# mLSTM into two MoE layers on one core: output gates by tanh, 1 + tanh in VectorE's product, and a new early order

## The chip, the cores and the metric

The kernel runs on one core of a Trainium2 chip. The metric is the device time in microseconds (us) of one execution. Engines are named as in the profile: PE is TensorE (matmuls), DVE is VectorE, ACT is ScalarE, POOL is GpSimd, SP is SyncE, which here issues most of the DMA transfers.

## The reference

The input is q, k, v (2 batches, 8 heads, 768 steps, 40 wide) and three gates. The first part is an mLSTM, the second a layer without a nonlinearity between its matrices but with a product, the third a layer with Mish. Everything is float32.

```python
for t in range(S):
    m_new = np.maximum(f_gate[:, :, t] + m, i_gate[:, :, t])
    f_stab = np.exp(f_gate[:, :, t] + m - m_new)
    i_stab = np.exp(i_gate[:, :, t] - m_new)
    m = m_new
    C = f_stab * C + i_stab * einsum('bhd,bhe->bhde', vt, kt)
    n = f_stab * n + i_stab * kt
    h_tilde = einsum('bhde,bhe->bhd', C, qt)
    denom = maximum(abs(n . qt), 1.0)
    o = 1.0 / (1.0 + exp(-o_gate[:, :, t]))
    y[:, :, t] = o * h_tilde / denom
x = y as 1536 tokens x 320
h = ((x @ w1) * (x @ w2)) @ w3 @ w_out     # 320 -> 1024 -> 1024 -> 320
h2 = h @ w_in                              # 320 -> 2048
out = (h2 * tanh(softplus(h2))) @ w_out2   # 2048 -> 320
```

## The kernel before

**Precision.** PE multiplies at full speed only in a rounded kind of float32 (`fp32r` in the rows). Where both factors are long, each is split into a high part that is exact in that kind and a low part, and a product is made of two or three matmuls. Splitting a weight tile (`add_piece`) takes a load (line 481), the magnitude (487 on ACT or 489 on DVE), a clamp (493), three bit operations (497, 502, 507) on DVE, the high part by ACT (512) and the low part by a subtraction (the helper `tt`, line 410) on DVE or POOL. All two-operand instructions that go through `tt` carry line 410; they are told apart by their tiles.

**Attention.** The 768 steps of a batch are cut into 6 chunks of 128; with 2 batches this gives 12 units u, chunk u // 2, batch u % 2. A unit goes through these steps, each a node of `add_unit`:

- `E` (623, 624, PE): exponents of the 128 x 128 decays into PSUM, two banks. For the first `mu` units a product with `causal` adds the mask (623); for the others POOL masks the result by an affine select (634). `dw` (629, ACT) takes the exponential and gives `w`.
- `S` (650, PE): the scores; `wg` (410, DVE, two halves): `w<-psS,w`, scores times decays.
- `vw` (410, POOL): values times the last decays; `U` (675, PE) and `st` (410, 692, DVE): the state that goes on to the next chunk of the batch; `I`, `dx`, `Ie` (661, 664, 639, 410): what comes from the state.
- `Y` (699, PE): 16 small matmuls in full fp32, `cb` (410 or 711, DVE): `y`, the numerator and the denominator. `r1` (716, ACT) its magnitude, `r2` (719, DVE) the maximum with 1, `r3` (722, DVE) the reciprocal.
- `xs` (410, POOL): `x<-y,sg`, the numerator times the output gate; `xo` (410, POOL): times `r`; `dup` (736, ACT); `X` (743, PE): transposition into `psX`; `Xe`, `Xl` (748 and 410): high part `hs`, low part `ls`.

The gates `sg` are loaded as six tiles of 2 chunks of a batch (`add_sigmoids`, 814: a sigmoid on ACT, two tiles and then four in a row). There are fewer places than tiles, so a later load waits until a tile has been read by `xs` of both its units. Sigmoid and exponential lie in different tables of ACT; whenever ACT goes from one to the other, a table is loaded.

**Start.** `start` computes the exponents' rows from the two gates on DVE by scans, for three pieces of the sequence (first, second and the other four chunks): `pa` (879), `pt` (410), `pb` (895), `pc` (900), `less` (927, DVE, what has to be subtracted), `lr` (905, ACT, a rounding), `ll` (410, DVE, its remainder), `rb` (919 or 410, `ex_r`) and `lb` (935, `ex_l`), the two factors of E.

**Layers.** Tokens go in 3 blocks of 512 (2 chunks of both batches). For each block the products A and B (1057, `psa`, `psb`, 8 slices of 128 of w1 and w2), `Ae` (1072, ACT) and `Be` (410, DVE, `a<-psb,a`), `Ph`, `Pl`. Once, the weights w3 and w_out are multiplied (W, 1028) from the parts `th` of w3 and `wol` of w_out; then X1 (1097 to 1102), and for groups of eight slices H (1186), Mish on ACT (1191, 1195), and O (1210), which is copied and stored.

**What sets the order.** The whole order is planned when the kernel is built: the class `Work` holds nodes with an engine, a length, what they need and what they free, and picks for each engine the ready node with the lowest due time. The due times of attention, of the first weights and of A and B come from a table of numbers (`DUE`), the choice of engines from `ENG`, other constants from `TUNE`. Where the plan expects PE to idle for long, it puts in fillers (`keep_warm`, 594: products of `causal` and `identr` into `psz` that nobody reads). Every engine then runs its instructions in the planned order, and so does SP its transfers.

Of the kernel before, what the change touches and what calls it, by code (L numbers as in the profile page):

```python
# [19 lines left out]
NQK = 2  # L20
# [6 lines left out]
    sgg=(2, 4), mu=8, s_pe=0.268, s_act=0.543, s_dve=0.435, s_pool=0.206, ahead=1, w0n=5, ff=0.972, gd=0.0,  # L27
    ph=0.071, a0=-12.81, ap=-93.853, a_ld=-1652.39, e_e=8363.2, e_s=3345.95, e_r=2252.59, g_ld=6316.58,
# [3 lines left out]
    c_o2=88.35, cp_o2=12.531, c_wi=-5894.32, c_o3=-2264.6, m0=232.0, grp=8, mp0=-162.897, mp=204.465, m_o=1263.83,  # L32
# [3 lines left out]
    mag_w12='ACT', mag_wo='ACT', mag_w3='ACT', mag_wi='DVE', mag_o2='DVE', mag_o3='DVE', lo_w12='DVE', lo_wo='DVE',  # L36
    lo_w3='POOL', lo_wi='POOL', lo_o2='DVE', lo_o3='DVE', xo='POOL', vw='POOL', dup='ACT', rb0='DVE', rc0='DVE',
    rb1='DVE', rc1='DVE', rb='ACT', rc='ACT', st0='DVE', cb0='DVE', prep='ACT', g_tt='DVE', g_ll='DVE',
    lo_w120='DVE', lo_w121='DVE', lo_w122='DVE', lo_w123='DVE', lo_w124='DVE', lo_w125='POOL', lo_w126='DVE',
# [25 lines left out]
    bits2_1=61.7, mag_3=32.5, X_3=47.0, X_2=46.7, r2_4=44.8, dw_7=46.5, vw_5=43.9, r3_4=46.6, U_4=46.2,
    clamp_3=34.4, Xe_3=46.9, U_5=41.3, wg_5=50.4, Xe_2=46.5, sgm_2=47.7, ld_qk_7=31.4, st_5=50.7, Y_5=50.2,
    vw_6=49.9, ld_kv_7=41.9, st_4=32.2, Xl_3=43.0, S_6=52.6, cb_5=61.2, Xl_2=50.6, E_8=20.7, r1_5=45.6, xs_4=51.3,
    sgm_3=51.8, sgm_4=51.8, sgm_5=51.8, wg_6=52.0, A_0=53.4, dw_8=53.9, xs_5=49.6, ld_kv_8=25.3, r2_5=31.3,
    bits1_3=47.6, r3_5=49.7, vw_7=60.1, B_0=55.3, bits2_3=65.5, Ae_0=45.8, bits_1=62.5, I_7=66.9, ld_kv_9=56.1,
# [284 lines left out]
def dve(n):  # L354
    return 0.07 + n / 960
# [991 lines left out]
```

## Time and profile before

| | before |
|---|---|
| median of 3 runs | 418.12 us (418.02 to 418.21) |
| the profiled execution | 418.2 us |
| its span, first to last instruction | 416.5 us |
| mean granted clock of PE | 0.998 |
| busy: PE, DVE, ACT, POOL | 409.5, 291.1, 197.7, 80.4 us |
| share of the span | 98%, 70%, 47%, 19% |

The rows further down give times in us from the first instruction. A row of a timeline or of the chain can hold several instructions in a row of the same kind (`x2`); its second number is then the time from the first's start to the last's end. PE takes up a matmul before the one ahead has ended, so the distance between two starts, not the length, is what one costs. What stands in brackets at a row's end is the time the engine stood idle before, and what ended it.

### The profile page before, as it was taken

Reading aid. Unit: us, or ns where it says so; the run is one execution under the profiler, and the core shown is the slowest. Engines: PE = TensorE matmul, PEld = TensorE weight load, DVE = VectorE, ACT = ScalarE, POOL = GpSimd, SP = SyncE. Lnnn points to the kernel's source line nnn. Section 1 sums busy time; section 2 is a strip of 40 time slices with the busy share of each in tenths; the row PEclk is TensorE's granted clock in tenths of the full one; section 3 lists DMA queues with packets and bytes.
Section 4 is the critical chain, followed back from the end, with each engine's and each line's share of the span. In section 5 each row is a group of like instructions: output and inputs, shape, how many; then the busy total and the mean of one; then the engine's idle time right before and its main releaser. Section 6 shows DMA issues by size and latency. Waiting matters only on the chain.

```text
span 416.5 us, 7129 instructions
## 1 busy us (share of the span) xinstructions
PE 409.5 (98%) x2815; PEld 359.8 (86%) x2815; DVE 291.1 (70%) x527; ACT 197.7 (47%) x381; POOL 80.4 (19%) x78
## 2 busy tenths in 40 slices
PE   8999999999999999999999999999999999999996
PEld 5689988798888899988888888989989999889995
DVE  7999999999899969779999987789231041330221
ACT  8787967444544444542644376157051161340430
POOL 3234264345102242431001132300000000000000
PEclk9999999999999999999999999999999999999999
DMA  7957744433313543445243253420100000100002
GB/s 238 324 178 220 239 119 153 139 97 127 114 50 102 168 136 101 150 139 166 65 104 87 64 127 90 164 63 2 65 0 2 0 2 2 63 2 0 2 2 64
DMA packets 30497, 40.88 MB, mean 98 GB/s; under 512 B 1856, under 2 KB 24640, under 8 KB 30464
## 3 DMA queue, kind: packets, MB, share of 16 engines
q1 hardware_dynamic: 29952, 39.95, 31.4%
q8 instruction: 22, 0.36, 0.4%
q10 hardware_dynamic: 512, 0.48, 0.4%
q14 instruction: 11, 0.09, 0.1%
HBM read 38.45 MB, written 1.97 MB: 97 GB/s over the span
## 4 chain that ended last, share of the span: by engine, by line
PE 93%; DVE 5%; DMA 1%; ACT 0%; issue 0%; DVEq 0%
PE pso L1210 21%; PE psh L1186 20%; PE psb L1057 11%; PE psa L1057 10%; PE psw L1028 7%; PE psY L699 5%; PE psS L650 3%; PE psx L1097 3%; PE psx L1099 3%; PE psx L1098 3%; PE psI L661 2%; PE psx L1102 1%; PE psx L1101 1%; PE psE L624 1%; DVE gates L410 1%; PE psX L743 1%
## 5 line engine op out<-in xcount | busy, mean ns | idle before, releaser
L410 DVE TENSOR_TENSOR gl<-u,gh 128x512 fp32r<-128x512 f32 x48 | 32.9, 691 | 68.7 <-ACT u L1195 68.7
L1191 ACT ACTIVATE gh<-psh 128x512 fp32r<-128x512 f32 x48 | 28.8, 601 | 79.5 <-PE psh L1186 79.4
L1186 PE MATMUL psh<-xd,wih 64*128 64x512 f32 x240 | 59.4, 395 | 0.0
L1186 PEld LDWEIGHTS psh<-xd,wih 64*128 64x128 f32 x240 | 43.1, 184 | 3.6 <-ACT u L1195 0.2
L1210 PE MATMUL pso<-wo,gh 128*128 128x320 f32 x192 | 42.6, 310 | 0.0
L1186 PE MATMUL psh<-hs,wih 64*128 64x512 f32 x144 | 41.6, 395 | 0.0
L502 DVE SCALAR_TENSOR_TENSOR f<-raw,f 128x640 int32<-128x640 int32 (+2 forms) x44 | 40.0, 908 | 0.9
L507 DVE SCALAR_TENSOR_TENSOR f<-raw,f 128x640 int32<-128x640 int32 (+2 forms) x44 | 37.7, 858 | 0.9
L410 POOL TENSOR_TENSOR th<-f,th 128x512 fp32r<-128x512 f32 x16 | 22.1, 1381 | 62.1 <-ACT th L512 59.1
L1210 PEld LDWEIGHTS pso<-wo,gh 128*128 128x128 f32 x192 | 32.0, 188 | 1.1 <-issue 1.1
L1186 PE MATMUL psh<-xd,wil 64*128 64x512 f32 x120 | 31.6, 391 | 0.0
L1186 PE MATMUL psh<-hs,wil 64*128 64x512 f32 x120 | 31.4, 391 | 0.0
L1210 PE MATMUL pso<-wo2h,gh 128*128 128x320 f32 x96 | 30.0, 312 | 0.0
L1210 PE MATMUL pso<-wo2h,gl 128*128 128x320 f32 x96 | 29.6, 309 | 0.0
L1210 PE MATMUL pso<-wo2l,gh 128*128 128x320 f32 x96 | 29.6, 309 | 0.0
L1210 PE MATMUL pso<-wo,gl 128*128 128x320 f32 x96 | 29.6, 309 | 0.0
L1057 PE MATMUL psa<-hs,w12h 128*128 128x512 f32 x72 | 28.9, 401 | 0.1
L1195 ACT ACTIVATE u<-psh 128x512 f32<-128x512 f32 x48 | 28.9, 603 | 0.0
L1057 PE MATMUL psb<-hs,w12h 128*128 128x512 f32 x72 | 28.3, 394 | 0.2 <-DVE y L410 0.2
L1186 PEld LDWEIGHTS psh<-hs,wih 64*128 64x128 f32 x144 | 25.7, 184 | 3.2 <-issue 1.3
L1028 PE MATMUL psw<-woh,th 128*128 128x320 f32 x128 | 28.5, 310 | 0.0
L493 DVE TENSOR_SCALAR f<-f 128x640 f32<-128x640 f32 (+2 forms) x44 | 23.6, 536 | 7.0 <-ACT f L487 6.3
(146 smaller groups left out, 1031.8 us busy)
## 6 DMA issues: line engine op xcount, KB each, us to landing
raw<-in_w_dram SPq DMA_DIRECT2D x16, 512.0 KB
raw<-in_w_out_dram SPq DMA_DIRECT2D x12, 640.0 KB
raw<-in_w_dram SPq DMA_DIRECT2D x16, 384.0 KB
raw<-in_w_in_dram SPq DMA_DIRECT2D x16, 320.0 KB
kv<-in_kv_dram SPq DMA_DIRECT2D x12, 324.0 KB
qk<-in_qk_dram SPq DMA_DIRECT2D x24, 160.0 KB
sg<-in_o_gate_dram SPq DMA_DIRECT2D x12, 160.0 KB
out_dram<-yo SPq DMA_DIRECT2D x9, 160.0 KB
```

Of the source, the lines that this page charges most:

```text
L410: return eng.tensor_tensor(out=o, in0=a, in1=b, op=op)
L493: nc.vector.tensor_scalar(out=ff, in0=ff, scalar1=HI_MIN, scalar2=HI_MAX, op0=ALU.max, op1=ALU.min)
L502: nc.vector.scalar_tensor_tensor(out=f, in0=t["raw"][:, :, 1], scalar=-0x40000000, in1=f, op0=ALU.bitwise_and, op1=ALU.bitwise_or)
L507: nc.vector.scalar_tensor_tensor(out=f, in0=t["raw"][:, :, 0], scalar=29, in1=f, op0=ALU.logical_shift_right, op1=ALU.bitwise_or)
L650: nc.tensor.matmul(t["S"][g][:, p * T:(p + 1) * T], lhsT=t["qk"][rows, 1, p, :], rhs=t["qk"][rows, 0, p, :], start=True, stop=True)
L699: nc.tensor.matmul(ps[:, h * VW:(h + 1) * VW], lhsT=t["w"][:, h, :], rhs=t["v"][:, h, :], start=True, stop=True)
L1028: nc.tensor.matmul(ps, lhsT=t[a][:, 0, c * 128:(c + 1) * 128], rhs=wo[b], start=(c0 + c + s == 0), stop=(c0 + c == KC - 1 and s == 2))
L1057: nc.tensor.matmul(ps, lhsT=a, rhs=b, start=(n == 0 and not begun), stop=(n == len(seq) - 1))
L1186: nc.tensor.matmul(mt[i + k]["ps"], lhsT=w[k][:, c], rhs=x[k][c], start=(n == 0 and c == 0), stop=(n == 2 and c == KC2 - 1))
L1191: nc.scalar.activation(out=t["gh"], in_=t["ps"], func=AF.Mish)
L1195: nc.scalar.activation(out=t["u"], in_=t["ps"], func=AF.Mish)
L1210: nc.tensor.matmul(ps, lhsT=t[a][:, sl], rhs=wo[b], start=(ft == 0 and n == 0), stop=(ft == KF2 - 1 and n == 2))
```

## The change

The output gate is computed as (1 + tanh(x/2)) / 2. Tanh lies in the exponents' table. ACT takes one gate tile at a time, as six nodes. The 1 + goes into the product with the numerator, which becomes one `scalar_tensor_tensor` on DVE in place of POOL's product (`x<-sg,y`, line 734 of the new kernel); the half goes into the denominator: `r2` doubles behind the maximum.

The engines of some low parts change: the 16 of w3 (`th`) from POOL to DVE, the four of w_out (`wol`) from DVE to POOL, one of w1 and w2 (`w12l`) from DVE to POOL. One unit more gets its mask on PE (`mu` 9). In the last block the Mish parts and the output copies may use other places. New constants of the planner (`ss`, `fb`, `sw`) and the groups given as a list leave the groups as they were. The table of due times is new, up to the weights of the second part of the early work.

```diff
 TUNE = dict(
-    sgg=(2, 4), mu=8, s_pe=0.268, s_act=0.543, s_dve=0.435, s_pool=0.206, ahead=1, w0n=5, ff=0.972, gd=0.0,
+    sgg=(1, 1, 1, 1, 1, 1), mu=9, s_pe=0.268, s_act=0.543, s_dve=0.435, s_pool=0.003, ahead=1, w0n=5, ff=0.972,
+    gd=0.26, ph=0.071, a0=-12.81, ap=-93.853, a_ld=-1652.39, e_e=8363.2, e_s=3345.95, e_r=2252.59, g_ld=6316.58,
...
 ENG = dict(
-    mag_w12='ACT', mag_wo='ACT', mag_w3='ACT', mag_wi='DVE', mag_o2='DVE', mag_o3='DVE', lo_w12='DVE', lo_wo='DVE',
-    lo_w3='POOL', lo_wi='POOL', lo_o2='DVE', lo_o3='DVE', xo='POOL', vw='POOL', dup='ACT', rb0='DVE', rc0='DVE',
...
+    lo_wo='POOL', lo_w3='DVE', lo_wi='POOL', lo_o2='DVE', lo_o3='DVE', xo='POOL', vw='POOL', dup='ACT', rb0='DVE',
...
 DUE = dict(
-    set_0=0.0, ld_o_0=0.6, ld_g=1.3, ld_qk_0=1.7, ld_kv_0=1.8, load_0=1.9, ld_o_1=4.6, lr_0=4.8, less_0=2.3,
-    ll_0=4.5, la1_0=5.1, la0_0=5.4, rb_0=5.6, one_0=5.7, lb0_0=40.7, lb1_0=6.2, pl_1=6.1, rc_0=6.4, pl_0=18.6,
+    set_0=0.0, ld_o_0=0.6, ld_g=1.3, ld_qk_0=1.7, ld_kv_0=1.8, load_0=3.5, ld_o_1=4.6, lr_0=4.8, less_0=2.3,
+    ll_0=1.9, la1_0=5.1, la0_0=5.4, rb_0=5.3, one_0=5.7, lb0_0=40.6, lb1_0=6.2, pl_1=6.1, rc_0=6.4, pl_0=19.4,
...
     def z_slot(name):
         tag = work.take()
+        if tag[0] == "y":
+            k, n = divmod(int(tag[1:]), 5)
+            h, l = xset["b", k]
+            return (h[:, n] if n < 3 else l[:, n - 3]).bitcast(F32)
...
         def r2():
-            nc.vector.tensor_scalar_max(out=t["r"], in0=t["r"], scalar1=1.0)
+            nc.vector.tensor_scalar(out=t["r"], in0=t["r"], scalar1=1.0, scalar2=2.0, op0=ALU.max, op1=mult)
...
         def xs():
             x = t["x"] = slot(att, "x", [128, 3 * T])
             xh = x[:, 0:DM].rearrange("a (h d) -> a h d", h=H)
-            tt(nc.gpsimd if ENG["xo"] == "POOL" else nc.vector, xh, t["y"][:, :, 0:D], sg[kb, b][:, j % 2], mult)
+            nc.vector.scalar_tensor_tensor(out=xh, in0=sg[kb, b][:, j % 2], scalar=1.0, in1=t["y"][:, :, 0:D], op0=add, op1=mult)
...
         def sgm():
             for i in which:
                 o = sg[divmod(i, B)]
-                nc.scalar.activation(out=o, in_=o, func=AF.Sigmoid)
-
-        add_node(("sgm", which[0]), "ACT", due, act(640) * len(which), sgm, [("ld_o", i) for i in which], table=["sig"])
+                nc.scalar.activation(out=o, in_=o, func=AF.Tanh, scale=0.5)
+
+        add_node(("sgm", which[0]), "ACT", due, act(640) * len(which), sgm, [("ld_o", i) for i in which], table=["exp"])
...
+        GP = places("z", 16) + (places("z", 6, 25) + places("y", 10)) * last
+        YP = places("z", 16) if last else places("z", 6, 25)
```

The built kernel has two loads of ACT's tables in place of six. Its lines are numbered up to 18 higher than before (line 410 is 412, 927 is 937, 594 is 600, 699 is 706, 587 is 593).

DVE in the start, on the way to the first factors of E. Before:

```order
L900 SCALAR_TENSOR_TENSOR gates<-gates 128x127
L927 SCALAR_TENSOR_TENSOR gates<-gates 64x128
L410 TENSOR_TENSOR gates<-gates 32x128
L410 TENSOR_TENSOR ex_r_90<-gates,sel_h 64x512
L935 SCALAR_TENSOR_TENSOR ex_l_89<-gates,neg_b,ex_l_89 32x128
```

And now:

```order
L910 SCALAR_TENSOR_TENSOR gates<-gates 128x127
L412 TENSOR_TENSOR gates<-gates 32x128
L937 SCALAR_TENSOR_TENSOR gates<-gates 64x128
L412 TENSOR_TENSOR ex_r_90<-gates,sel_h 64x512
L945 SCALAR_TENSOR_TENSOR ex_l_89<-gates,neg_b,ex_l_89 32x128
```

`ll` (32x128), which needs ACT's rounding, has changed places with `less` (64x128), which doesn't.

DVE ahead of the fourth w product, the last row of each (`f` are steps of splitting a weight tile, `st_80` is the state of batch 0, `y` the numerators). Before:

```order
L410 TENSOR_TENSOR w12l<-f,w12h 128x768
L493 TENSOR_SCALAR f<-f 128x768
L722 RECIPROCAL r<-r 128x8
L410 TENSOR_TENSOR st_80<-st_80,d 128x328
L410 TENSOR_TENSOR st_80<-psU,st_80 40x4x41 x2
L410 TENSOR_TENSOR y<-psY,y 128x328
L493 TENSOR_SCALAR f<-f 128x768
L497 TENSOR_SCALAR f<-f 128x768
L410 TENSOR_TENSOR ls_139<-psX,hs_138 128x2x128
L410 TENSOR_TENSOR hs_138<-psX,hs_138 64x128
L502 SCALAR_TENSOR_TENSOR f<-raw,f 128x768
L410 TENSOR_TENSOR w<-psS,w 128x4x128 x2
```

And now:

```order
L729 RECIPROCAL r<-r 128x8
L412 TENSOR_TENSOR w12l<-f,w12h 128x768
L412 TENSOR_TENSOR y<-psY,y 128x328
L734 SCALAR_TENSOR_TENSOR x<-sg,y 128x320
L412 TENSOR_TENSOR st_80<-st_80,d 128x328
L412 TENSOR_TENSOR st_80<-psU,st_80 40x4x41 x2
L499 TENSOR_SCALAR f<-f 128x768
L503 TENSOR_SCALAR f<-f 128x768
L726 TENSOR_SCALAR r<-r 128x8
L508 SCALAR_TENSOR_TENSOR f<-raw,f 128x768
L729 RECIPROCAL r<-r 128x8
L412 TENSOR_TENSOR w<-psS,w 128x4x128 x2
```

The second `x<-sg,y` and a second pair of `r` stand ahead of the fourth w product now (the first `x<-sg,y` is further up), and the remainders `ls`, `hs` of the first transposition have moved up.

PE ahead of the fourth Y product, the last row of each (`psz` are fillers). Before:

```order
L743 MATMUL psX<-ident,x 128x128 x3
L650 MATMUL psS<-qk_79 128x128 x8
L661 MATMUL psI<-st_81,qk_79 128x82 x4
L664 MATMUL psI<-ex_r_91,ones_93 128x8
L675 MATMUL psU<-vw,kv 40x41 x8
L743 MATMUL psX<-ident,x 128x128 x3
L594 MATMUL psz<-causal,identr 128x512 x4
L699 MATMUL psY<-kv,w 128x41 x8
```

And now:

```order
L657 MATMUL psS<-qk_79 128x128 x8
L668 MATMUL psI<-st_81,qk_79 128x82 x4
L671 MATMUL psI<-ex_r_91,ones_93 128x8
L682 MATMUL psU<-vw,kv 40x41 x8
L600 MATMUL psz<-causal,identr 128x512 x8
L706 MATMUL psY<-kv,w 128x41 x8
```

The first transposition now stands ahead of the third Y, the second behind the fourth; the three fillers that stood ahead of the third Y are gone, and eight stand here.

## Rows read from the trace of the kernel before

**Rows 1.** Windows: start:end, length; busy PE, PEld, DVE, ACT, POOL; clock, DMA, GB/s.

```profile
18.00:50.00 32.00, 31.88 (x336) 28.61 (x334) 30.14 (x68) 26.15 (x65) 11.61 (x13) 1.00 0.72 215
50.00:110.00 60.00, 59.71 (x469) 50.93 (x469) 56.89 (x110) 32.75 (x70) 26.65 (x25) 1.00 0.40 123
110.00:240.00 130.00, 130.00 (x637) 111.44 (x636) 115.14 (x195) 60.80 (x103) 25.25 (x18) 1.00 0.37 115
```

**Rows 2.** Waits of PE: tile and line, releaser, us in total, times, longest.

```profile
PE psb L1057 <- DVE y L410: 0.2, 1, 0.2
```

**Rows 3.** Chain of work that ended last, 32 to 46 us: start, us, what.

```profile
32.82 0.33 PE psX L743 x3
...
36.24 0.93 PE psz L594 x4
37.17 1.72 PE psY L699 x16
...
41.08 0.34 PE psE L623
...
43.01 0.74 PE psU L675 x32
43.75 1.91 PE psY L699 x16
```

**Rows 4.** Timeline of DVE, 24 to 38 us: start, us, line, operation.

```profile
24.52 0.56 DVE L497 TENSOR_SCALAR f<-f 128x768 int32<-128x768 int32 x1
...
31.15 0.45 DVE L410 TENSOR_TENSOR st<-st,d 128x328 f32<-128x328 f32 x1
31.71 0.67 DVE L410 TENSOR_TENSOR st<-psU,st 40x164 f32<-40x164 f32 x2
32.40 0.50 DVE L410 TENSOR_TENSOR y<-psY,y 128x328 f32<-128x328 f32 x1
32.82 0.55 DVE L493 TENSOR_SCALAR f<-f 128x768 f32<-128x768 f32 x1
33.41 1.05 DVE L497 TENSOR_SCALAR f<-f 128x768 int32<-128x768 int32 x1
...
35.77 1.27 DVE L410 TENSOR_TENSOR w<-psS,w 128x512 f32<-128x512 f32 x2
36.97 0.19 DVE L719 TENSOR_SCALAR r<-r 128x8 f32<-128x8 f32 x1
37.20 0.20 DVE L722 RECIPROCAL r<-r 128x8 f32<-128x8 f32 x1
37.32 0.45 DVE L410 TENSOR_TENSOR y<-psI,eT 128x328 f32<-128x328 f32 x1
```

**Rows 5.** Timeline of DVE in the start.

```profile
5.02 0.28 DVE L927 SCALAR_TENSOR_TENSOR gates<-gates 64x128 f32<-64x128 f32 x1
5.35 0.29 DVE L410 TENSOR_TENSOR gates<-gates 32x128 fp32r<-32x128 f32 x1
5.67 0.69 DVE L410 TENSOR_TENSOR ex_r<-gates,sel_h 64x512 fp32r<-64x512 f32 x1
```

**Rows 6.** Timeline of ACT in the start.

```profile
5.02 0.29 ACT L905 CAST gates<-gates 64x128 fp32r<-64x128 f32 x1 [0.19 <-DVE gates L900]
```

**Rows 7.** Timeline of POOL, 33 to 48 us.

```profile
33.23 0.81 POOL L410 TENSOR_TENSOR x<-y,sg 128x320 f32<-128x320 f32 x1 [0.34 <-PE psX L743]
...
47.82 0.75 POOL L410 TENSOR_TENSOR vw<-kv,w 128x328 f32<-128x328 f32 x1 [1.44 <-DMA kv<-in_kv_dram]
```

**Rows 8.** Timeline of SP's queue, 34 to 43 us: start and length of the issue.

```profile
34.06 1.24 SPq L587 DMA_DIRECT2D sg<-in_o_gate_dram  x2
...
36.14 0.35 SPq L587 DMA_DIRECT2D kv<-in_kv_dram  x1
39.21 0.92 SPq L481 DMA_DIRECT2D raw<-in_w_dram  x2
...
42.83 0.42 SPq L587 DMA_DIRECT2D kv<-in_kv_dram  x1
```

More of the change, by code (lines that the diff above doesn't have):

```diff
@@ L65 @@
[L65 to L69, printed above, removed]
@@ L296, in plan @@
                     s0 = min(c[0] for c in cand)
[L297 removed]
+                    stay = TUNE["fb"] if e == "PE" else 0.0
+                    c = min((c for c in cand if c[0] <= s0 + TUNE.get(SLACK.get(e), 0.0)),
+                            key=lambda c: c[1] - (stay if self.form[c[2]] == form else 0.0))
                     if pick is None or c[0] < pick[0]:
@@ L322, in plan @@
             if e == "PE" and self.form[n] != form:
-                last += self.SWITCH
+                last += TUNE["sw"]
                 form = self.form[n]
@@ L645, in S_ @@
         def S_():
-            t["S"] = [bank("psS") for _ in range(2)]
-            for p in range(HP):
-                for g in range(2):
-                    rows = slice(64 * g, 64 * g + D)
-                    nc.tensor.matmul(t["S"][g][:, p * T:(p + 1) * T], lhsT=t["qk"][rows, 1, p, :],
-                                     rhs=t["qk"][rows, 0, p, :], start=True, stop=True)
+            for t in (tl[x] for x in mine):
+                t["S"] = [bank("psS") for _ in range(2)]
+                for p in range(HP):
+                    for g in range(2):
+                        rows = slice(64 * g, 64 * g + D)
+                        nc.tensor.matmul(t["S"][g][:, p * T:(p + 1) * T], lhsT=t["qk"][rows, 1, p, :],
+                                         rhs=t["qk"][rows, 0, p, :], start=True, stop=True)
         def wg():
@@ L764, in add_unit @@
         node("dw", "ACT", -K["e_e"] + 1, 2 * act(512), dw, [("E", u)], table=["exp"])
-        node("S", "PE", -K["e_s"], 0.9, S_, [("ld_qk", u), ("E", u), ("Y", u - K["ahead"])], [at("wg"), at("wg")],
-             warm=0.45, form=1)
+        mine = [x for x in range(u - u % B, u - u % B + B)] if c >= K["ss"] else [u]
+        if u == mine[0]:
+            node("S", "PE", -K["e_s"], 0.9 * len(mine), S_,
+                 [(x, n) for n in mine for x in ("ld_qk", "E")] + [("Y", u - K["ahead"])],
+                 [(AT, [("wg", n)]) for n in mine for _ in range(2)], warm=0.45, form=1)
         if not pe_mask:
             node("ms", "POOL", -K["e_e"] + 2, 0.13 + 1016 / 1130, ms, [("dw", u)])
-        node("wg", "DVE", -3, 2 * dve(512), wg, [("S", u), ("dw", u), ("vw", u), ("ms", u)])
+        node("wg", "DVE", -3, 2 * dve(512), wg, [("S", mine[0]), ("dw", u), ("vw", u), ("ms", u)])
         if c > 0:
@@ L791, in add_unit @@
         last = pool(320) - 0.03 if xo_e == "POOL" else dve(320)
-        node("xs", xo_e, 1, last, xs, [("cb", u), ("sgm", kb * B + b)], [(places("x", 2), [("X", u)])], port=True)
+        node("xs", "DVE", 1, dve(320), xs, [("cb", u), ("sgm", kb * B + b)], [(places("x", 2), [("X", u)])], port=True)
         node("xo", xo_e, 2, last, xo, [("xs", u), ("r3", u)], port=True)
@@ L1154, with group @@
     MH = places("b", 4)
-    GP, UP, YP = places("z", 16), places("z", 4, 16), places("z", 6, 25)
+    UP = places("z", 4, 16)
+    def group(i):
+        return next((a, b) for a, b in zip(K["grp"], K["grp"][1:]) if a <= i < b)
     acc = {}
@@ L1270 @@
             wo2_n[2 * i], wo2_n[2 * i + 1] = (n, 0), (n, 1)
-        G = K["grp"]
-        dues = [K["m0"] + (i // G) * G * 3.49 + (i % G) * 1.72 for i in range(NT)]
+        dues = [K["m0"] + group(i)[0] * 3.49 + (i - group(i)[0]) * 1.72 for i in range(NT)]
         for i in range(KF1):
```

122 lines of the change are left out of this document (64 added, 58 removed).

## The prediction

> **What bounds the kernel now.** I read the busy times by stretch first. From 18 us to 240 us PE is busy 31.88 of 32.00 us, 59.71 of 60.00 and 130.00 of 130.00 [rows 1]: behind the start, PE sets the time, and there is 0.12 + 0.29 us in which it does nothing. The table of what PE waits for agrees: it has four rows, three of which lie in the start; the fourth, 0.2 us for a gate product, stands in [rows 2]. So work taken off another engine can hardly gain anything; what changes the time is work put on PE, and waits put in front of it.
>
> A busy PE is not a useful PE, though. The chain of work that ended last shows four filler products (`psz`) of 0.93 us from 36.24 to 37.17, ahead of the fourth Y product [rows 3]; three more stand before the third Y. Fillers are put where the order expects PE to wait, and here it waits for DVE: the fourth w product (`w<-psS,w`, two halves) starts at 35.77 and its last half is over at 36.97, when the next DVE instruction starts [rows 4], and Y follows at 37.17. From 18 to 38 us DVE hands PE its work with no slack. In 18 to 50 us DVE is busy 30.14 of 32 us [rows 1], so whatever is added to DVE before 37 us shows on PE one for one; after 50 us PE has the products of A and B to go on with.
>
> **The change part by part.** The base is the median, 418.12 us; the profiled execution, at 418.2 us for a span of 416.5, is 0.1 above it, and its differences are used as they stand.
>
> *1. The start.* `ll` now stands ahead of `less` on DVE. In the trace `less` starts at 5.02, `ll` at 5.35, the first `ex_r` at 5.67 [rows 5], and ACT's rounding that `ll` needs (line 905) runs from 5.02 for 0.29 us [rows 6], beside `less`. Exchanged, DVE stands idle while ACT rounds: `ll` can't start before about 5.33, `less` follows at 5.65 and `ex_r` at 5.98, 0.31 us later. DVE has no idle time from there to the first w product, so all behind is 0.31 us late.
>
> *2. DVE up to the fourth w product.* By the order of the built kernel, between the first and the fourth w product DVE gets two products `x<-sg,y` more (those of units 0 and 1, taken from POOL) and one more pair of max and reciprocal for `r`; the clamps, bit operations and low parts there are the same in number. The nearest row for the new product has the same output to within 8 columns: `y<-psY,y`, 0.42 us from its start to the next (32.40 to 32.82) [rows 4]. Two cost 0.84. The pair costs 0.35 (36.97 to 37.32) [rows 4]. Against it stands what POOL's product did to DVE: at 33.41 a `f<-f` of 128x768 took 1.05 us beside POOL's `x<-y,sg` at 33.23 [rows 7], and 0.56 at 24.52 with POOL idle [rows 4]: 0.49 comes back. With the start, 0.31 + 0.84 + 0.35 - 0.49 = **+1.0 us** for the fourth Y, which begins at 38.0 in place of 37.01 (as the records give it). Bounds: +0.3 if DVE's idle 1.86 us of 18 to 50 [rows 1] absorb 0.7 of it, +1.5 if no stretch comes back. The eight fillers now in one row before this Y, 8 x 0.23 = 1.86 us, fit into the wait: 0.93 were there, a transposition (`psX`, 0.33 [rows 3]) moved from before it to behind, and the rest is the lateness. They cost nothing of their own.
>
> *3. The SyncE queue.* The gates' tiles are loaded into places that free when `x<-y,sg` of the second unit has read them. The load at 34.06 was released by POOL's product (33.23 + 0.81) [rows 7, 8]. In the new kernel it waits for DVE's third `x<-sg,y`, which stands behind the fourth w product (from 36.77), `y<-psI,eT` and both steps of `st`: 1.20 + 0.45 + 0.56 + 0.69 + 0.42 [rows 4] = 3.3, so about 40.0. Queued behind this load are the q/k and the kv loads of unit 5; kv went out 2.08 us after it, at 36.14 [rows 8], and now goes at 42.1. POOL's `vw` needs that kv. The same three loads before, with kv at 42.83, gave a `vw` at 47.82 that had waited for it: 5.0 us [rows 7, 8]. That would be `vw` at 47.1, done at 47.8, and PE comes to unit 5's U at 46.2 (38.0, and 8.1 us of work between as in the chain: from 37.17 to 43.75, less half of U's 0.74, and the fifth Y's 1.91 [rows 3]): +1.6. But ahead of those loads went a weight load at 39.21 [rows 8], which is now behind them; without it kv may be on time. I take the half, **+0.8**, between 0 and 1.6.
>
> *4. Work on PE.* One unit more gets its mask by two products (0.23 each, as the fillers of the same shape: 0.93 for four [rows 3]), in place of an affine select on POOL: 0.46, behind Y_5. One transposition, 0.33, is moved behind Y_5 and has still to be done (Y_5 is the Y of unit 5, the sixth). A product in full fp32 followed by one of the rounded kind takes about 0.1 more (0.34 for the first mask behind I, at 41.08 [rows 3], where 0.23 is usual); the new order has one such change fewer before Y_5 and two more after: 0.2. Filler 39 for 38 is in step 2. From Y_5 to the end **+1.0 us**, almost fixed: this much nobody can hide, since PE has no idle time to take it up.
>
> *5. What the other engines get rid of.* ACT loads four activation tables less and POOL its twelve gate products; but PE hardly waits for either. All that can come back from 50 to 110 us is the 0.29 us [rows 1]; I take **-0.3**, between -0.3 and 0.
>
> *6. What costs nothing.* `th`'s 16 low parts go to DVE, at 0.64, half of a pair `w<-psS,w` of the same shape [rows 4], 10 us, from 110 to 240 us, where DVE has 130 - 115.14 = 14.9 us to spare [rows 1], and four `wol` leave it; a low part that comes late in spite of this costs one 0.64. A w12 low part on POOL, the maximum that doubles too (one instruction as before), and the wider buffers of the last block leave the order of PE behind 215 us as it was.
>
> Sum: 1.0 + 0.8 + 1.0 - 0.3 = +2.5: 418.12 + 2.5 = **420.6 us**.
>
> **The rivals.** *Not slower.* Place: DVE from 18 to 37 us. With the table loads gone ACT hands DVE its magnitudes and masks sooner, and DVE's 1.86 us of idle time there [rows 1] shrink by what part 2 adds; the gate load is then out early enough for U. Steps 2 and 3 fall to nothing, 4 and 5 remain: 418.12 + 1.0 - 0.3 = 418.8. It decides from the point at which the fourth Y starts by 37.3. Against it: DVE starts its instructions between these products back to back [rows 4], so that the idle time lies elsewhere in the stretch; for it: PE has fillers there that can give way. To end below 417.3 it would need 0.8 us beyond all of that, and the rows show only 0.4 of PE idle: hardly to be had.
>
> *The two-input product stands still beside POOL.* `x<-sg,y` reads two tiles of SBUF. If it can't run while POOL reads there, each of the early ones waits for a `vw`, 0.75 [rows 7]: two before the fourth Y, +1.5, 422.1; if only the 0.49 of the stretched row, +1.0. For it: the row of 1.05 us. Against: POOL has lost just the instruction that stretched it. The Trainium skill, page "SBUF — State Buffer", section "Who interferes with whom", has this as a rule: a DVE instruction with two SBUF inputs contends with a GpSimd instruction that reads SBUF. By it the sum would be this rival's. No row here decides it: the operation of 1.05 us has one tile as its input, and none with two tiles stands beside POOL by itself.
>
> *kv later still.* If the load of unit 5 takes the 5.0 us and the later ones slip as well, step 3 is 1.6 and more: 421.4 to 422.
>
> That the change doesn't do what it says can be excluded for the tables: the built kernel has two table loads for six.
>
> **How the numbers follow.** A measurement of this kernel tells 0.2% (0.84 us) from no change; the bounds are 417.28 and 418.96. Forecast (419.2 to 421.6): 0.47. Not slower: 0.25, of which 0.06 below 417.3 for what the rows don't show. Contention: 0.15. kv: 0.13. So faster 0.06, same 0.19, slower 0.75. The range goes from 418.5, within the rival that is not slower, to 421.9: some 0.1 stays out on either side.
>
> **What would show it.** First `ex_r` at 5.98 for 5.67. The fourth Y at 38.0 with eight fillers before it (right), at 37.3 or before (the first rival). The load of gates that was at 34.06 at about 40, unit 5's kv at 42, and PE waiting for `vw` before that U (step 3); `x<-sg,y` at 0.5 us or above 1 us (contention). From Y_5 to the end 1.0 us more. If PE behind the fourth Y meets operands that come earlier than before, I am wrong.

## The result, and the profile after

| | before | after |
|---|---|---|
| median, same chip | 418.21 us (418.02 to 418.35) | 421.35 us (420.19 to 428.52) |
| ratio | 1 | 1.0066, 95% interval 1.0047 to 1.0085 |
| profiled execution | 418.2 us, span 416.5 | 421.35 us, span 419.5 |
| mean granted clock of PE | 0.998 | 0.993 |
| busy PE, DVE, ACT, POOL | 409.5, 291.1, 197.7, 80.4 us | 411.8, 296.5, 192.4, 53.4 us |

Executions over 1.5% above the fastest of their kernel (here the one of 428.52 us, at a mean clock of 0.973) are left out of the ratios; the kernel before had none among 71, the new kernel one and nine of the twelve experiments one to five each.

By the ratio the change costs 2.8 us. The two executions of the new kernel in which the mean clock was 0.999 took 420.19 and 420.47 us, so 2.0 to 2.3 us of it are there without a fall of the clock; the profiled one, at 0.993, shows what a fall adds. ACT lost 5.3 us of work and POOL 27, as the change says, and neither paid anything back. Where the time went is read from the stretches first (start:end and length, then the busy times of PE, PEld, DVE, ACT and POOL, the granted clock, DMA). They answer to [rows 1]:

```profile
18.00:50.00 32.00, 31.39 (x311) 27.17 (x310) 30.24 (x64) 21.13 (x55) 5.83 (x7) 0.95 0.63 192
50.00:110.00 60.00, 60.00 (x482) 52.21 (x481) 57.15 (x118) 30.48 (x70) 21.47 (x19) 1.00 0.41 134
110.00:240.00 130.00, 130.00 (x641) 111.81 (x640) 117.81 (x210) 61.69 (x107) 9.72 (x6) 1.00 0.38 116
```

PE is busy throughout behind 50 us, so everything was lost before, and in 18 to 50 us the granted clock is 0.95 for 1.00. Cut finer:

```profile
18.00:21.00 3.00, 2.59 (x22) 2.16 (x21) 2.94 (x7) 0.67 (x2) 0.00 (x0) 1.00 1.04 275
21.00:24.50 3.50, 3.50 (x21) 2.84 (x20) 3.41 (x7) 1.48 (x6) 0.00 (x0) 0.56 0.76 261
```

From 21 to 24.5 us PE ran at the lower of its two levels (1.2 for 2.4 GHz). What it did before is in its timeline (start, time to the end of the row's last matmul, line, operation):

```profile
15.67 2.59 PE L600 MATMUL psz<-causal,identr 128*128 128x512 f32 x10 [0.31 <-ACT eT L957]
18.49 0.42 PE L706 MATMUL psY<-kv,w 128*128 128x41 f32 x2 [0.23 <-DVE w L412]
19.09 1.75 PE L706 MATMUL psY<-kv,w 128*128 128x41 f32 x14 [0.18 <-DVE w L412]
20.78 1.54 PE L657 MATMUL psS<-qk 40*128 40x128 f32 x16
```

It stood still twice ahead of and in the first Y, then had only the small matmuls of Y and S; the fall follows. In the chain of work that ended last (start, us, what) the price can be read off, since before the fall and after it the same products stand in one row of the chain:

```profile
19.09 1.75 PE psY L706 x14
20.85 1.47 PE psS L657 x16
22.32 0.72 PE psE L629
23.04 0.43 PE psE L630
23.47 0.43 PE psE L629
...
25.30 0.23 PE psE L630
```

A 512-column product takes 0.43 us instead of 0.23. The second Y starts at 25.91, 2.20 us later than before (23.71): 0.73 because the larger part of the first Y starts at 19.09 for 18.36, the other 1.47 behind it, where the same products stand in another order, by the clock. The fourth Y then starts at 39.31 for 37.01, and its last 14 matmuls at 39.91 for 37.16, 2.75 late; the sixth Y is 2.93 late, the first H 2.62, the last matmul 2.64, and the end of the span 3.0.

DVE's timeline shows both reasons for the late first Y. It answers to [rows 5] and [rows 4]:

```profile
5.36 0.29 DVE L412 TENSOR_TENSOR gates<-gates 32x128 fp32r<-32x128 f32 x1 [0.36 <-ACT gates L915]
5.68 0.28 DVE L937 SCALAR_TENSOR_TENSOR gates<-gates 64x128 f32<-64x128 f32 x1
5.99 0.69 DVE L412 TENSOR_TENSOR ex_r<-gates,sel_h 64x512 fp32r<-64x512 f32 x1
...
16.40 1.32 DVE L945 SCALAR_TENSOR_TENSOR ex_l<-gates,neg_b,ex_l 32x512 fp32r<-32x512 f32 x1
17.75 1.29 DVE L412 TENSOR_TENSOR w<-psS,w 128x512 f32<-128x512 f32 x2
...
26.72 0.91 DVE L734 SCALAR_TENSOR_TENSOR x<-sg,y 128x320 f32<-128x320 f32 x1
...
34.64 0.49 DVE L734 SCALAR_TENSOR_TENSOR x<-sg,y 128x320 f32<-128x320 f32 x1
...
38.57 1.29 DVE L412 TENSOR_TENSOR w<-psS,w 128x512 f32<-128x512 f32 x2
```

`ex_r` at 5.99 is step 1 of the prediction (5.98). But `ex_l` at 16.40 takes 1.32 us, and took 0.74 before (at 16.25). In POOL's timeline its neighbours stand, and those of the first `x<-sg,y`, which took 0.91 for the 0.49 of the second:

```profile
16.43 0.75 POOL L412 TENSOR_TENSOR vw<-kv,w 128x328 f32<-128x328 f32 x1 [5.15 <-DMA kv<-in_kv_dram]
26.54 0.75 POOL L412 TENSOR_TENSOR vw<-kv,w 128x328 f32<-128x328 f32 x1 [9.37 <-ACT w L635]
```

SP's queue answers to [rows 8]. The gate tile that was loaded at 34.06 goes at 35.87, not at 40, and the kv load of unit 5 at 38.38; PE takes its U at 48.07 without a wait:

```profile
35.42 0.36 SPq L593 DMA_DIRECT2D kv<-in_kv_dram  x1
35.87 1.62 SPq L593 DMA_DIRECT2D sg<-in_o_gate_dram  x2
37.59 0.70 SPq L616 DMA_DIRECT2D qk<-in_qk_dram  x2
38.38 0.35 SPq L593 DMA_DIRECT2D kv<-in_kv_dram  x1
```

### The profile page after: what moved, and what is told of

The parts are those of the page before. It is cut to its first block, busy times and chain, and to the rows that moved or that the text cites. A ratio compares the mean times of both kernels' runs of the same rounds, so it can differ in the third digit from the quotient of the medians.

```text
span 419.5 us, 7117 instructions
## 1 busy us (share of the span) xinstructions
PE 411.8 (98%) x2818; PEld 361.1 (86%) x2818; DVE 296.5 (71%) x550; ACT 192.4 (46%) x377; POOL 53.4 (13%) x54
## 4 chain that ended last, share of the span: by engine, by line
PE 93%; DVE 4%; DMA 1%; issue 1%; ACT 0%; DVEq 0%
PE pso L1225 20%; PE psh L1201 20%; PE psa L1067 11%; PE psb L1067 10%; PE psw L1038 7%; PE psY L706 5%; PE psS L657 3%; PE psx L1107 3%; PE psx L1109 3%; PE psx L1108 3%; PE psI L668 2%; PE psx L1112 1%; PE psx L1111 1%; PE psE L630 1%; PE psX L750 1%; PE psE L629 1%
## 5 line engine op out<-in xcount | busy, mean ns | idle before, releaser
L412 DVE TENSOR_TENSOR gl<-u,gh 128x512 fp32r<-128x512 f32 x42 | 28.8, 691 | 62.6 <-ACT u L1210 62.5
L1206 ACT ACTIVATE gh<-psh 128x512 fp32r<-128x512 f32 x42 | 25.2, 600 | 75.3 <-PE psh L1201 75.2
L508 DVE SCALAR_TENSOR_TENSOR f<-raw,f 128x640 int32<-128x640 int32 (+2 forms) x44 | 39.7, 903 | 0.8
L513 DVE SCALAR_TENSOR_TENSOR f<-raw,f 128x640 int32<-128x640 int32 (+2 forms) x44 | 35.5, 806 | 0.9
L493 ACT ACTIVATE f<-raw 128x512 f32<-128x512 f32 (+2 forms) x28 | 21.4, 763 | 21.0 <-DVE th L412 8.7
L412 POOL TENSOR_TENSOR wil<-f,wih 128x640 fp32r<-128x640 f32 x8 | 13.9, 1752 | 127.6 <-ACT wih L518 127.6
L1201 PE MATMUL psh<-ls,wih 64*128 64x512 f32 x96 | 26.3, 390 | 0.0
L706 PEld LDWEIGHTS psY<-kv,w 128*128 128x128 f32 x192 | 23.0, 192 | 2.2 <-DVE w L412 1.7
L1225 PE MATMUL pso<-wo2h,gl 128*128 128x320 f32 x80 | 24.7, 309 | 0.0
```

Source lines behind the costliest of these rows:

```text
L412: return eng.tensor_tensor(out=o, in0=a, in1=b, op=op)
L493: nc.scalar.activation(out=t["f"].bitcast(F32), in_=t["raw"][:, :, 1].bitcast(F32), func=AF.Abs)
L508: nc.vector.scalar_tensor_tensor(out=f, in0=t["raw"][:, :, 1], scalar=-0x40000000, in1=f, op0=ALU.bitwise_and, op1=ALU.bitwise_or)
L513: nc.vector.scalar_tensor_tensor(out=f, in0=t["raw"][:, :, 0], scalar=29, in1=f, op0=ALU.logical_shift_right, op1=ALU.bitwise_or)
L706: nc.tensor.matmul(ps[:, h * VW:(h + 1) * VW], lhsT=t["w"][:, h, :], rhs=t["v"][:, h, :], start=True, stop=True)
L1201: nc.tensor.matmul(mt[i + k]["ps"], lhsT=w[k][:, c], rhs=x[k][c], start=(n == 0 and c == 0), stop=(n == 2 and c == KC2 - 1))
```

## The experiments

The theories: the product on DVE makes PE wait before the fourth Y (step 2); the start makes it wait before the first; and, new after the result, these stops let the granted clock fall, which adds to their price. Against them stand the order as such, the table loads and the tail. Each ratio below is against the kernel before on the same chip; its medians there were 418.25 to 418.5. In the experiments on the order the planned order is edited before the instructions are issued; nothing else changes (`...` stands for the exchange or the fillers, which each section shows):

```diff
         self.plan(t0, fill)
-        for s, _, n in sorted(self.order):
+        seq = [n for _, _, n in sorted(self.order)]
+        ...
+        for n in seq:
```

### The arithmetic alone, in the old order

```diff
-                nc.scalar.activation(out=o, in_=o, func=AF.Sigmoid)
+                nc.scalar.activation(out=o, in_=o, func=AF.Tanh, scale=0.5)
...
-            nc.vector.tensor_scalar_max(out=t["r"], in0=t["r"], scalar1=1.0)
+            nc.vector.tensor_scalar(out=t["r"], in0=t["r"], scalar1=1.0, scalar2=2.0, op0=ALU.max, op1=mult)
...
-            tt(nc.gpsimd if ENG["xo"] == "POOL" else nc.vector, xh, t["y"][:, :, 0:D], sg[kb, b][:, j % 2], mult)
+            nc.vector.scalar_tensor_tensor(out=xh, in0=sg[kb, b][:, j % 2], scalar=1.0, in1=t["y"][:, :, 0:D], op0=add, op1=mult)
```

> The kernel before with the arithmetic of the gates alone: tanh, the doubling in `r2`, and `x<-sg,y` on DVE at the place in the order where POOL's product was issued. Every other instruction keeps its place; ACT loads two tables for six. Theory (step 2 of the prediction): DVE carries 0.84 us more ahead of the fourth w product and gets some of POOL's stretch back, so the fourth Y starts 0.3 to 0.8 us later than 37.02 and the time is 418.6 to 419.1 us, with the clock held. Rival (the lighter ACT and POOL pay for it): 417.9 to 418.3. If the new order is what costs, this kernel stays below 419.

Measured: 421.4 us, ratio 1.0070 (1.0057 to 1.0083). The fourth Y starts at 37.88, 0.87 late, just above the 0.3 to 0.8 of the theory, with the four fillers in front of it as before. But 419.1 was too low by 2: what is late there goes on. DVE's timeline, up to the fourth w product:

```profile
32.70 0.67 DVE L410 TENSOR_TENSOR st<-psU,st 40x164 f32<-40x164 f32 x2
33.40 0.50 DVE L410 TENSOR_TENSOR y<-psY,y 128x328 f32<-128x328 f32 x1
33.81 0.55 DVE L493 TENSOR_SCALAR f<-f 128x768 f32<-128x768 f32 x1
34.40 0.56 DVE L497 TENSOR_SCALAR f<-f 128x768 int32<-128x768 int32 x1
34.87 0.48 DVE L727 SCALAR_TENSOR_TENSOR x<-sg,y 128x320 f32<-128x320 f32 x1
35.28 0.42 DVE L410 TENSOR_TENSOR ls<-psX,hs 128x256 fp32r<-128x256 f32 x1
...
36.67 1.27 DVE L410 TENSOR_TENSOR w<-psS,w 128x512 f32<-128x512 f32 x2
```

The product costs 0.41 from start to start (34.87 to 35.28), the prediction's 0.42 from `y<-psY,y`, and L497 is back from 1.05 to 0.56 us. Later the clock fell here too, at another place, behind the fifth Y and its S:

```profile
48.00:51.00 3.00, 3.00 (x13) 2.61 (x12) 2.97 (x7) 2.53 (x7) 0.87 (x1) 0.50 0.63 176
```

### The product on DVE, without tanh

```diff
-            tt(nc.gpsimd if ENG["xo"] == "POOL" else nc.vector, xh, t["y"][:, :, 0:D], sg[kb, b][:, j % 2], mult)
+            tt(nc.vector, xh, t["y"][:, :, 0:D], sg[kb, b][:, j % 2], mult)
```

> The kernel before with the product `x<-y,sg` on DVE alone; the gate stays a sigmoid with its own table, six table loads. Theory (the product on DVE is what costs): as with the whole arithmetic in the old order, the fourth Y at 37.6 to 37.9 and 420.2 to 421.4 us. Rival (it was tanh and its doubling, or their places on ACT): 418.2 to 418.8.

Measured: 420.37 us, ratio 1.0047 (1.0031 to 1.0062). The sigmoid and its table loads are all there, and the time is still 2.0 us up, so it is the product's move. In its trace the clock holds, and the lateness can be followed: fourth Y 0.63 (37.64), the same at the sixth, 1.37 at the twelfth, 1.61 at the first W. Two fifths of that are lost before the fourth Y, as step 2 has it, another 0.86 from the eleventh Y at 93 us to the first W, where the prediction had nothing. It is DVE again: the chain that ended last runs over DVE from 91.08 to the twelfth w product, but for one step of ACT, and two of the moved products stand in it:

```profile
93.63 0.40 DVE x L410
...
100.40 0.39 DVE x L410
...
101.47 1.21 DVE w L410 x2
102.72 1.76 PE psY L699 x14
```

The last 0.4 of the span's 2.0 lies behind the last matmul (see the tail below).

### The gate whole on ACT

```diff
-                nc.scalar.activation(out=o, in_=o, func=AF.Sigmoid)
+                nc.scalar.activation(out=o, in_=o, func=AF.Tanh, scale=0.5)
+                nc.scalar.activation(out=o, in_=o, func=AF.Copy, scale=0.5, bias=0.5)
```

> The kernel before, the gate by tanh in the exponents' table, but made whole on ACT: tanh, then times 0.5 plus 0.5 in a second instruction; POOL keeps its product `x<-y,sg`, DVE is as before, nothing else is moved. Four table loads less, six instructions more on ACT. Theory (the cost of the change lies in DVE's product, and the tables were off the path): 418.1 to 418.4, the fourth Y at 37.0. Rival (tables on the path): 417.3 to 417.8. A second rival (tanh's own path costs, by its place or by the clock): 419 and more.

Measured: 419.5 us, ratio 1.0032 (1.0017 to 1.0048). The fourth Y is at 37.00, as before, and all is on time up to the seventh: the four table loads less give nothing, and DVE without the product is not late. What is lost comes from this kernel's own edit. Four tiles in a row, two instructions each, hold ACT for 5.74 us, and PE then waits for ACT ahead of a transposition (0.37 at 67.07) and is 0.8 late at the eighth Y; 0.6 of it reaches the last matmul:

```profile
49.13 5.74 ACT L814 ACTIVATE sg<-sg 128x640 f32<-128x640 f32 x8
```

So the second rival is half right: tanh has a price by its place on ACT. It is not the price of the change, which takes one tile at a time.

### The new order without the product on DVE

The new kernel with the edit of the section before and `x<-y,sg` back on POOL, `r2` without the doubling.

> The new kernel with the gate made whole on ACT (tanh, then times 0.5 plus 0.5) and the product back on POOL, `r2` without the doubling; the new order, masks and fillers stay. Theory (DVE's product makes the waits before the first and fourth Y longer, the order as such costs 0.5 to 1): 418.8 to 419.6 with few falls of the clock. Rival (the new order costs by itself, since it was laid out for other lengths): 420 and more, with falls up to 428.

Measured: 423.16 us, ratio 1.0089 (1.0061 to 1.0118). The measurement is the rival's: the order gives nothing back where the product's length is taken out of it. The first Y starts at 18.28, the clock falls at 21 us as in the new kernel, and its fourth Y is at 39.5. By the ratios the product alone costs 2 us (1.0047), this kernel 3.7 (1.0089) and both together 2.8 (1.0066), so the two don't add up. What the order costs by itself is not shown: ACT's second instruction, which cost 1.3 us in the old order (1.0032), is in this kernel too.

### The start, alone and undone

```diff
+        seq.remove(("ll", 0)); seq.insert(seq.index(("less", 0)), ("ll", 0))
```

> The kernel before with one exchange alone: `ll` ahead of `less` on DVE, all else in the old order. Theory (start and clock): the first w product comes 0.3 us or more later (more if the ex_l row at 16.25 meets POOL's `vw` as it does in the new kernel, where it took 1.32 us for 0.74), PE stands still before the first Y, and in most executions the clock falls: 418.5 to 420.3. Rival: 418.5 in all of them, with the clock at 1.00 throughout.

Measured: 418.66 us, ratio 1.0001 (0.9992 to 1.0010): no difference that these executions can tell, though `ex_r` starts at 5.98. Of the 0.31 us 0.16 reach the first Y (18.10 for 17.94), and this stays to the end. DVE gives half of it back on the way to the first w product (`ex_l` at 16.39 for 16.25). PE's first Y is late by too little to stand still, and the clock holds. And the other way round, in the new order:

```diff
+        seq.remove(("less", 0)); seq.insert(seq.index(("ll", 0)), ("less", 0))
```

> The new kernel with one exchange undone: `less` stands ahead of `ll` on DVE again, all else in the new order. Theory (start and clock): the first `ex_r` starts at 5.67 instead of 5.99, PE's first Y no longer stands still twice behind its fillers (0.23 and 0.18 us in the new kernel), and the granted clock stays at its upper level from 21 to 25 us; 0.3 to 0.7 us come back from the start and in those executions in which the clock had fallen another 1.4: about 419.7 at the median. Rival (the order behind): the exchange is worth its 0.3 us alone, about 421.

Measured: 420.9 us, ratio 1.0049 (1.0032 to 1.0067), `ex_r` back at 5.67; the intervals of the two kernels overlap, so this says at most that the exchange is worth little. In its profiled execution the clock fell earlier, at 15.4 us, behind the small `psg` products of the start. The place of the fall is not fixed.

### The clock: taking fillers away, and adding them

The kernel before with three fillers less ahead of its first Y; nothing that computes is moved or made to wait.

```diff
+        i = max(j for j in range(seq.index(("Y", 0))) if isinstance(seq[j], int))
+        seq[i] -= 3
```

> The kernel before with 7 fillers instead of 10 ahead of the first Y: PE stands still for 0.7 us from 17.2 to 17.9, while nothing that computes is moved. Theory (clock): the granted clock falls behind it as in the new kernel and the time goes up by 1.4 us to 419.6 in all or most executions. Rival (standing still costs nothing there): 418.2.

Measured: of twelve executions five took 418.23 to 418.75 us, two 421.54 and 421.71 (mean clock 0.991), and five 425.76 to 432.35 (0.963 to 0.979), where the 23 of the kernel before on that chip end at 419.84. The ratio, which leaves the last five out, is 1.0018 (0.9996 to 1.0040), unclear by itself. Taking 0.7 us of work away that nobody reads lets PE stand still, and in some executions this costs 3 us and more. In the profiled one, of 418.23 us, the clock held after stops of 0.39 and 0.18 us. The theory has the direction, not the size: where the clock fell, it cost more than 1.4 us. In the new kernel, with 14 fillers for 10 (`seq[i] += 4`):

> The new kernel with 14 fillers instead of 10 ahead of the first Y, all else in the new order; PE then works until 19.2 us, 0.1 later than the second half of the first w product is ready, and does not stand still before the first Y. Theory (clock): the granted clock does not fall behind the first Y in any execution, so 420.3 us, with a spread as small as that of the kernel before. Rival (the clock falls for another reason, such as the scores and masks that now follow the first Y directly): as before the edit, 420.2 to 423, or 0.1 more.

Measured: 423.32 us, ratio 1.0080 (1.0052 to 1.0108). A miss: covering the stops at the first Y alone doesn't hold the clock. There are others: in the fourth Y PE stands still as well (0.18 in the trace after, at 39.91). In this kernel's own trace, of 427.6 us, the first Y runs through and no fall follows it; the fourth stands still for 0.18 at 38.31, and the clock is at its lower level from 41.1 to 58.2 us. With 14 fillers there and 11 for 8 ahead of the fourth Y:

```diff
+        i = max(j for j in range(seq.index(("Y", 0))) if isinstance(seq[j], int))
+        seq[i] += 4
+        i = max(j for j in range(seq.index(("Y", 3))) if isinstance(seq[j], int))
+        seq[i] += 3
```

> The new kernel with 14 fillers for 10 ahead of the first Y and 11 for 8 ahead of the fourth, all else unchanged, so that PE stands still ahead of neither. Theory (standing still inside these light stretches makes the clock fall): no execution falls; 420.6 to 421 in all of them. Rival (the fall needs no standing still: the new order has longer stretches of small matmuls): again some executions at 423 to 428, as with 14 fillers alone.

Measured: 420.34 us, ratio 1.0055 (1.0042 to 1.0068), six executions from 419.70 to 421.69; none with a large fall, though the two slowest have a mean clock of 0.994 and 0.995. Seven fillers, 1.6 us of work, were added, and the ratio is 0.0011 (0.5 us) below the new kernel's; the two intervals overlap, so that a gain is not shown. The windows of the profiled execution: no idle time on PE, and the clock at 1.00.

```profile
18.00:50.00 32.00, 32.00 (x329) 28.57 (x328) 30.72 (x66) 22.77 (x59) 6.49 (x7) 1.00 0.69 207
50.00:110.00 60.00, 60.00 (x480) 52.16 (x480) 57.16 (x119) 29.92 (x68) 21.08 (x19) 1.00 0.40 131
```

With the start undone and 12 and 11 fillers:

```diff
+        seq.remove(("less", 0)); seq.insert(seq.index(("ll", 0)), ("less", 0))
+        i = max(j for j in range(seq.index(("Y", 0))) if isinstance(seq[j], int))
+        seq[i] += 2
+        i = max(j for j in range(seq.index(("Y", 3))) if isinstance(seq[j], int))
+        seq[i] += 3
```

> The new kernel with `less` ahead of `ll` again, 12 fillers for 10 ahead of the first Y and 11 for 8 ahead of the fourth. Theory (start 0.3 us, stops of PE and the clock on top of what DVE's product costs): no execution with a large fall, the fastest at 419.4, the median at 419.5 to 420.1, 0.3 to 0.8 below the kernel with more fillers alone. Rival (the start is worth nothing behind the fillers): 420.3 as with more fillers alone. Both leave the fourth Y at 37.6 or later, since DVE's two products ahead of it remain.

Measured: 420.18 us, ratio 1.0036 (1.0024 to 1.0047), the fastest 419.58; the fourth Y at 38.05. The median is just above what the theory expected (419.5 to 420.1) and just below the rival's 420.3, and one of nine executions was at 427, so the clock is not held for certain. This is the best that was found for the new kernel, 1.5 us above the kernel before.

### One exchange on PE, and the last block's places

```diff
+        seq.remove(("S", 1)); seq.insert(seq.index(("E", 2)) + 1, ("S", 1))
```

> The new kernel with one exchange on PE: the scores of unit 1 stand behind the exponents of unit 2 again, as before, so that four 512-column products come between the first Y and the scores. Theory (a long stretch of small matmuls lets the clock fall at 21 us): no fall at 21 us, and fewer or smaller ones in all; 420.2 to 420.6 at the median. Rival (the falls come from the waits and their phase, not from this place): the same spread as the new kernel, 420.2 to 428.

Measured: 421.39 us, ratio 1.0086 (1.0061 to 1.0110). The times are the rival's (420.94 to 428.08), but the test is inconclusive on the clock: with the exponents ahead of the scores PE waits 0.67 us at 21.6 us for DVE's `ex_l`, which stands later in the new order, so the exchange brings a stop of its own. In the profiled execution the clock held all the same.

```diff
-        GP = places("z", 16) + (places("z", 6, 25) + places("y", 10)) * last
-        YP = places("z", 16) if last else places("z", 6, 25)
+        GP = places("z", 16)
+        YP = places("z", 6, 25)
```

> The new kernel with the places of the last block's Mish parts and output copies as before. In the traces the time from PE's end to the end of the span is 4.4 us with the new places and 4.0 with the old. Theory (the tail belongs to the places): 0.35 us come back, the fastest executions at 419.8. Rival (the tail is chance or has another cause): 420.2 as the fastest, tail 4.4.

Measured: 420.58 us, ratio 1.0044 (1.0031 to 1.0057), the tail as long as in the new kernel (4.4 us behind the last matmul), as the rival has it, so the places don't make the tail. The fastest executions, 419.68 and 419.70, are the theory's 419.8 all the same; where that comes from is not shown. The profiled execution shows the clock's part best, beside the one with more fillers ahead of the same Y. Here PE, with eight fillers, stood still inside the fourth Y:

```profile
37.51 0.42 PE L706 MATMUL psY<-kv,w 128*128 128x41 f32 x2
38.10 1.76 PE L706 MATMUL psY<-kv,w 128*128 128x41 f32 x14 [0.18 <-DVE w L412]
39.79 1.40 PE L657 MATMUL psS<-qk 40*128 40x128 f32 x16
```

and the clock fell for seven microseconds behind it:

```profile
37.00:40.00 3.00, 2.79 (x21) 2.20 (x21) 2.85 (x7) 0.91 (x4) 1.60 (x2) 1.00 0.85 247
40.50:47.00 6.50, 6.50 (x39) 5.87 (x38) 4.27 (x9) 3.32 (x8) 1.85 (x2) 0.51 0.70 217
```

In the kernel with eleven fillers the same Y ran through and the clock stayed:

```profile
35.64 2.79 PE L600 MATMUL psz<-causal,identr 128*128 128x512 f32 x11
38.27 1.88 PE L706 MATMUL psY<-kv,w 128*128 128x41 f32 x16
```

The pair doesn't prove that the stop is the cause: the same stop of 0.18 in the fourth Y stands in the new kernel (39.91) and in three others with its order (38.66, 39.67 and 40.09), and no fall follows it there.

## Why the prediction was right, and where it was not

The direction and the size came out (420.6 forecast, within 418.5 to 421.9; 421.35 measured), but the sum is made of other terms than forecast. The nearness is luck in part: steps 3 and 4, 1.8 of the 2.5 forecast, came to less than 0.1, and in the profiled execution 1.47 of the clock and 0.4 at the end of the span, which no step had, stood in their place.

- **Bound.** Right: PE stays busy behind 50 us, and what ACT and POOL lost bought nothing.
- **Step 1, the start.** `ex_r` came at 5.98 to 5.99 as forecast; its price was mis-sized. Alone it puts the first Y 0.16 later, not 0.31, and no measurable time on the whole.
- **Step 2, DVE up to the fourth w product.** Right in the mechanism, and shown by the move alone: 0.63 with the product, 0.87 with all of the arithmetic. In the old order three products stand ahead of that place and no pair of `r` more, so the step's own terms give 3 x 0.41 - 0.49 = 0.74; the 0.41 per product and the 0.49 that come back at L497 are in the trace. In the new kernel, with 1.47 of the clock taken off, the late part of the fourth Y is 1.3 late, against 1.0; 0.58 of that is the stretched `ex_l` ahead of the first Y, which the step did not have.
- **Step 3, the queue.** Wrong. The second, not the third, `x<-sg,y` on DVE is that of unit 2, which frees the tile (34.64, and the load follows at 35.87). I read the order of units off the order of rows, which have no unit in their names. 0.8 became 0.
- **Step 4, PE's own work.** Mis-sized: +1.0 behind the sixth Y was "almost fixed". From there to the first W at 146.3 us the lateness grew by 0.06. The two masks and the filler are there, 0.69 in all; but the step counted one kind of neighbours only. The other direction costs too, a rounded product followed by S: from start to start 0.33 for 0.23, as these rows of PE before the change show. Of such places behind exponents the old order has four, the new one has one; with the products of A and B it is six and four.

```profile
20.50 0.39 PE L623 MATMUL psE<-causal,identr 128*128 128x512 f32 x1
20.73 0.40 PE L624 MATMUL psE<-ex_r,ex_l 128*128 128x512 f32 x1
21.06 1.16 PE L650 MATMUL psS<-qk 40*128 40x128 f32 x16
```

Counted with the distances of before for every pair of neighbours, PE's work from the first Y to the first W is 0.1 us more in the new order, not 0.8.

- **Step 5.** The 0.29 of idle time from 50 to 110 us did come back (60.00 of 60.00), and another 0.37 between the first W and the first H, so the low parts that were moved between DVE and POOL (step 6) show no cost there.
- **The rivals.** Contention, priced at 1.0 to 1.5, took part: 0.42 at the first `x<-sg,y`, and 0.58 at `ex_l`, an instruction that I had not looked at. The prediction says that no instruction with two tiles stands beside POOL by itself; one does, in the trace before: `ex_l` at 16.25, with `vw` at 16.52, which took 1.07 for the 0.75 of others. The rival that wasn't written down is the granted clock, 1.47 of the 3.0 us in the profiled execution and, by the two executions at 0.999, next to nothing in others. The prediction's "busy PE is not a useful PE" went only as far as fillers being waste. The sum had no term for a stop of PE beyond its own length.
- **Tail.** From the last matmul to the end of the span it is 4.4 us for 4.0 in most later kernels, the old places included; with the new places and the product on POOL it is 4.0. It is not explained.

## What to carry to other kernels

An engine that frees itself of work gains nothing where it isn't waited for; look at the one that takes the work over, and at the next instruction on it that PE waits for: here a product of 0.41 us, two or three times ahead of such an instruction, was worth 0.6 to 0.9 there, and the tables' 5.1 us were worth nothing. Where PE is kept busy by fillers, a stop of a few tenths can be followed by a fall of the clock that costs several times its length, so plan fillers by the latest time at which the operand may come (what this gains was not clear of noise here), and time a change of the order by many executions, not by the fastest. To see which buffer a load waits for, follow the unit through the order; rows of one name say nothing of it.

## What the runs showed of the hardware

**The clock and stops of PE.** In six of the profiled executions PE went to the lower of its levels: at 21.4 us (new kernel, and new order with the product on POOL), 15.4, 40.5, 41.1 and 47.9 us. Ahead of five of these it had stood still for 0.18 to 0.6 us in all, among small matmuls; ahead of the one at 47.9 no stop is listed, only U, Y and S in a row, as in the kernel before at 42.9, where no fall follows. But stops without a fall are as many: the two ahead of 15.4 us (0.27 and 0.31) stand in the trace of the kernel before as well, 0.18 in the fourth Y in four traces, 0.39 and 0.18 with three fillers less, and 0.67 in the kernel with the exchange on PE. A fall cost 1.47 us in the new kernel and about 3.1 behind 40.5 us (9.95 us from the fourth to the fifth Y for the new kernel's 6.85). With the same program it falls or not: with fewer fillers in the old order, 421.71 and 418.23 on one chip. That stops make it likelier is what the fillers taken away speak for (seven of twelve executions above 421.5 us, none of 23 without the edit); the fillers added point the same way, within the noise. What decides it in one execution stays open.

**Two-input instructions beside POOL.** `ex_l<-gates,neg_b,ex_l` of 32x512 has two tiles of SBUF as inputs. It took 0.74 us wherever POOL's `vw` began 0.05 us or more behind it, 1.12 where `vw` was already running, and 1.32 in the new kernel, where both began within 0.03 us; in the first case `vw` was the longer one. Here both cases, in the old order with the arithmetic alone, and with the product alone:

```profile
16.24 0.74 DVE L935 SCALAR_TENSOR_TENSOR ex_l<-gates,neg_b,ex_l 32x512 fp32r<-32x512 f32 x1
```

```profile
16.74 0.85 POOL L410 TENSOR_TENSOR vw<-kv,w 128x328 f32<-128x328 f32 x1 [5.06 <-DMA kv<-in_kv_dram]
```

```profile
16.07 1.12 DVE L935 SCALAR_TENSOR_TENSOR ex_l<-gates,neg_b,ex_l 32x512 fp32r<-32x512 f32 x1
```

```profile
15.79 0.86 POOL L410 TENSOR_TENSOR vw<-kv,w 128x328 f32<-128x328 f32 x1 [4.84 <-DMA kv<-in_kv_dram]
```

Which of them comes first is set by when kv lands, so 0.4 to 0.6 us of the first w product's time are a matter of the execution: the kernels with 14 fillers and with the old places, whose order up to there is the new kernel's on DVE and POOL, took 0.74 for its 1.32. The Trainium skill, page "SBUF — State Buffer", section "Who interferes with whom", states that a DVE instruction with two SBUF inputs contends with a GpSimd instruction that reads SBUF. By that rule, the traces agree: `ex_l` loses 0.38 to 0.58 us beside a `vw` of 0.75 to 0.9.
